# A recurrence's triangular solve spread over more of its group, and the first T of each group placed on chip

## The chip, the cores and the metric

The kernel runs on one core of one Trainium2 chip. The metric is the device time of one execution in microseconds (us). The engines are named as in the profile: PE is TensorE (PEld its weight loads), DVE is VectorE, ACT is ScalarE, POOL is GpSimd, SP is SyncE, which issues most DMAs here.

## What is computed

Three stages follow each other. The first is a recurrence over 768 steps for 4 x 8 heads of 40 x 40 state; the second routes each of the 3072 rows of its output to two of eight experts; the third is a feed-forward layer. The change is in the first alone.

```python
for t in range(S):                      # S = 768
    y[:, :, t] = np.einsum('bhd,bhde->bhe', rt, state)
    Sa = np.einsum('bhde,bhe->bhd', state, at)
    state_decay = state * wt[:, :, None, :] - np.einsum('bhd,bhe->bhde', Sa, bt)
    state = state_decay + np.einsum('bhd,bhe->bhde', vt, kt)
x = y.transpose(0, 2, 1, 3).reshape(B * S, H * D)
x = moe(x)                              # top 2 of 8 experts
return (g(x @ w_in) @ w_out)            # g(h) = h * tanh(softplus(h))
```

## The kernel before, in words

The 768 time steps are cut into 24 chunks of 32 (`C`). Inside a chunk the recurrence becomes matrix products with a triangular 32 x 32 matrix L for each head, and its inverse T. Four chunks (`GJ`) make a group k, and the six groups' T are found by a forward substitution on VectorE, the solve. Five pieces of work run side by side:

- The chain (`chain`), 48 steps, two for each chunk (half of the heads each). A step has on TensorE the products that carry the state (`s_mm`, matmuls cs of ST and KB, L602), two sets of transposes (`tr`, L619), the product u (`u_mm`, L589), the output of the step before (`y_mm`, L559) and rv (`rv_mm`, L634). ScalarE copies u to ST (L592) and the transposes to TRs and KB (L621, L623). VectorE writes RR (L645) and the new ST (L607) for the two steps on.
- The preparation of later chunks (`prepare`): decays E and R, and abd and kb on VectorE (L227 to L240); L (matmuls pp, L280; ACT Ls, L287), stored to the DRAM tile lscr (L288); kn (L314) and EN (L325).
- The solve (`solve_group`), one group ahead of the chunks that need it. SyncE loads L of four chunks from lscr to Lu (L437). VectorE works on Lu and Tt (multiply L466 or L478, sum L468 or L481), and GpSimd takes two of the multiplications. The finished Tt is stored to the DRAM tile tscr (L517).
- The placing of T (`tbd`): T of one chunk is loaded from tscr with four DMAs into the block diagonal of Tbd (L384). There are two Tbd buffers (`NTB`).
- The application (`apply`): TensorE multiplies AM by Tbd (matmuls pp of Tbd and share, L406) and ScalarE copies the result to Zt (L408), which the chain's u needs.

The order of the instructions on each engine is fixed when the program is built. `run` walks through the steps of the chain and, at up to five places in a step (`fill`), issues all side work that is due by then (`pump`). Due times are counted in groups: a group is eight steps. The solve of group k goes from `k - 1 + s[0]` to `k - 1 + s[1]` (`s_1` for k = 1), and its load of Lu is due `ll` = 0.06 ahead. Each engine then takes its instructions in this order and waits where an operand is not ready.

For k = 0 alone, at the start, `own_tbd` makes T of the first chunk without DRAM: VectorE transposes 32 partitions of Tt in 32 x 32 blocks (L374), and ScalarE copies the result to the four diagonal blocks (L378).

Of the kernel before, what the change touches and what calls it, by code (L numbers as in the profile page):

```python
# [24 lines left out]
PR = 8  # L25
NC = S // C
NG = NP * NC
OPT = dict(yd=(), yv=33, gix=(1, 3, 4), ye=(2, 2),  lag2=1, plan=((0, 4, -0.881), (1, 5, -0.7929), (1, 6, -0.7905), (0, 5, -0.3416), (1, 7, -0.3331), (0, 6, -0.2825), (0, 7, -0.1981), (1, 8, -0.1391)), dl=0, dk=0, ns=(0, 0), nw=(1, 1), va=1, rb=0, ra=1, kb=0, ry=(2, 2), p1=(0, 0, 0, 1, 1, 1), lw=((4, 2, 2), (6, 6, 6)), fl=((0, 1, 2, 2, 2, 2, 2, 2), (0,) * 8), lag=6, ll=.06, hurry=40, pool=(1, 4), rvpool=False, f=(3, 3, 1, 1, 1, 0), s=(.05, .72), s_1=(-.12, .62), tl=1.9, zl=.96, zd=.32, t0=-.35, nd=3, z0=8.65)
NW = 2 * PR * (C + 1)
NTB = 2  # L30
GJ = 4
# [34 lines left out]
class Rec:  # L66
# [200 lines left out]
    def prods(self, i):  # L267
# [18 lines left out]
        for out, k in ((ls, 1), (am[:, :, 64:96], 0))[:1 if i < GJ else 2]:  # L286
            nc.scalar.mul(out=out, in_=pv[:, :, k], mul=-1.0)  # L287
        (nc.scalar if i < OPT['dl'] else nc.sync).dma_start(out=self.lscr[i // GJ][i % GJ * PR:i % GJ * PR + PR].rearrange("u q t i -> (q t) u i"), in_=ls)  # L288

# [12 lines left out]
    def turns(self, i):  # L302
# [12 lines left out]
        self.KN[i] = self.pkn.tile([128, HH * D], F32, name="knd")  # L315
        (nc.scalar if i < OPT['dk'] else nc.sync).dma_start(out=self.KN[i], in_=kn.rearrange("p h d -> p (h d)"))
        if i % 2 == 0:
# [28 lines left out]
    def prepare(self):  # L346
        n = len(self.seq)
        for first, i, at in OPT["plan"]:
            yield at
            for k, _ in enumerate((self.decayed if first else self.turned)(i)):  # L350
                yield at if first or at < OPT["t0"] else at + .03 * k
        for i in range(2 * GJ, n):
# [14 lines left out]
        for k in range(len(self.seq) // GJ):  # L367
            yield from self.solve_group(k)

    def own_tbd(self):  # L370

        nc = self.nc
        tv = self.ptm.tile([128, C * C], F32, name="tm")
        nc.vector.transpose(out=tv[0:32].rearrange("p (t x) -> p t x", x=32),  # L374
                            in_=self.Tt[0:32, 0:C * C].rearrange("p (j t) -> p t j", t=C))
        for q in range(4):
            r = slice(32 * q, 32 * q + 32)
            nc.scalar.copy(out=self.Tbd[0][r, :, r], in_=tv[0:32].rearrange("p (t u q) -> p q u t", u=PR, q=4)[:, q])  # L378

    def tbd(self, i):  # L380

# [5 lines left out]
    def apply(self):  # L387

        nc = self.nc
        for i in range(len(self.seq)):  # L390
            at = 2 * i - OPT["zl"]
            if i and i % GJ == 0:
                yield self.tau(2 * i - OPT["tl"])
                self.tbd(i)
            self.wants[2] = lambda: 2 if self.solved <= i // GJ else self.ready <= i
            z = self.Z[(i + 2) % 3]
            am, T = self.AM[i % (2 * GJ)], self.Tbd[i % NTB]
            if i < GJ:
                yield self.tau(at) if i else self.early(OPT['z0'])
                self.halves(i, am, T)  # L400
                T = self.IG
            for sg in range(2):
                yield self.tau(at + sg * OPT["zd"]) if i else self.early(OPT['z0'])
                pt = self.pp.tile([128, 512], F32, name="pp")
                for p in range(4):
                    nc.tensor.matmul(pt[0:96, p * 128:p * 128 + 128], lhsT=am[:, sg * 4 + p],  # L406
                                     rhs=T[:, sg * 4 + p, :], start=True, stop=True)
                nc.scalar.copy(out=z[0:96, sg * 4:sg * 4 + 4].rearrange("p a x -> p (a x)"), in_=pt[0:96])  # L408
            self.ZT[i] = z
            if 0 < i % GJ < GJ - 1 or i and i % GJ == 0:  # L410
                self.tbd(i + 1)
# [28 lines left out]
    def solve_group(self, k):  # L440

        nc = self.nc
        done = [0.0]

        def at(cost):

            done[0] += cost
            if k == 0:
                return self.early(done[0] - cost)
            return s0 + (s1 - s0) * (done[0] - cost) / 21.0  # L450

        s0, s1 = (k - 1 + x for x in OPT["s"]) if k != 1 else OPT["s_1"]
        if k:
            self.wants[1] = lambda: self.made < GJ * (k + 1)
            yield s0 - OPT["ll"]
            self.load_l(k)
        Tt, Lu = self.Tt, self.Lu
        q, h = C // 2, C // 4
        blk = lambda t: t[:, 0:4 * (h * C + h)].rearrange("p (b x) -> p b x", b=4)[:, :, 0:h * C].rearrange(
            "p b (j t) -> p b j t", t=C)  # L460
        Tb, Lb = blk(Tt), blk(Lu)
        for t in range(1, h):
            yield at(.38 + .0083 * t * t)
            tm = self.ptm.tile([128, 2 * C * q], F32, name="tm")
            tm = tm[:, 0:4 * t * t].rearrange("p (b j i) -> p b j i", b=4, j=t)
            nc.vector.tensor_tensor(out=tm, in0=Tb[:, :, 0:t, 0:t],  # L466
                                    in1=Lb[:, :, t, None, 0:t].to_broadcast([128, 4, t, t]), op=ALU.mult)
            nc.vector.tensor_reduce(out=Tb[:, :, 0:t, t:t + 1], in_=tm, axis=AX.X, op=ALU.add)  # L468
        T2 = Tt[:, 0:C * C].rearrange("p (j t) -> p j t", t=C)
        L2 = Lu[:, 0:C * C].rearrange("p (t i) -> p t i", i=C)  # L470
        P = self.one.tile([128, q, q], F32, name="P")
        work, tms = {}, {}

        def mul(i, eng=nc.vector):
            sh, x, y, _ = work[i]
            tm = self.ptm.tile([128, 2 * C * q], F32, name="tm")
            tms[i] = tm[:, 0:sh[0] * sh[1] * sh[2]].rearrange("p (a b c) -> p a b c", a=sh[0], b=sh[1])
            eng.tensor_tensor(out=tms[i], in0=x.to_broadcast([128, *sh]), in1=y.to_broadcast([128, *sh]), op=ALU.mult)  # L478

        def add(i):  # L480
            nc.vector.tensor_reduce(out=work[i][3], in_=tms.pop(i), axis=AX.X, op=ALU.add)  # L481


        for b in range(2):
            o = b * q
            p = P[:, 4 * b:4 * b + 4].rearrange("p a (c x) -> p (a c) x", x=h)
            work[b] = ((h, h, h), T2[:, o:o + h, None, o:o + h], L2[:, None, o + h:o + q, o:o + h], p[:, :, :, None])
            work[2 + b] = ((h, h, h), T2[:, o + h:o + q, o + h:o + q].rearrange("p i t -> p t i")[:, None],
                           p[:, :, None, :], T2[:, o:o + h, o + h:o + q, None])
        for i in range(0, 4, 2):  # L490
            for f in (mul, add):
                for b in range(2):
                    yield at(.6)
                    f(i + b)

        tt = self.T22
        for n, (j0, j1, i0) in enumerate(((0, 4, 0), (4, 8, 0), (8, 16, 8)) if k else ()):
            work[n] = ((j1 - j0, q, q - i0), T2[:, j0:j1, None, i0:q], L2[:, None, q:C, i0:q], P[:, j0:j1, :, None])
        for n, (t0, t1, j0, j1) in enumerate(((8, 16, 0, 8), (8, 16, 8, 16), (0, 8, 0, 16)) if k else ()):
            nt = t1  # L500
            work[3 + n] = ((j1 - j0, t1 - t0, nt),
                           tt[:, None, t0:t1, 0:nt], P[:, j0:j1, None, 0:nt], T2[:, j0:j1, q + t0:q + t1, None])
        pool = OPT["pool"] if k else ()
        for i in range(2 if k else 0):
            yield at(.1 if i in pool else 1.2)
            mul(i, nc.gpsimd if i in pool else nc.vector)
        for i in range(6 if k else 0):
            yield at(1.2)
            add(i)
            if i == 1:  # L510
                nc.scalar.copy(out=tt, in_=T2[:, q:C, q:C].rearrange("p i t -> p t i"))

            for j in {0: [2], 2: [4, 3], 3: [5]}.get(i, []):
                yield at(.1 if j in pool else 1.2)
                mul(j, nc.gpsimd if j in pool else nc.vector)
        self.tscr[k] = self.pd.tile([GJ * PR, 4, C, C], F32, name="tscr")
        (nc.sync if k else nc.scalar).dma_start(out=self.tscr[k].rearrange("u q j t -> (u q) (j t)"), in_=self.Tt[:, 0:C * C])  # L517
        self.solved += 1
        if k == 0:
            self.own_tbd()  # L520
            self.tbd(1)


# [1241 lines left out]
```

## Time and profile before

| | |
|---|---|
| median of 3 runs | 1275.37 us (1272.05 to 1279.73) |
| profiled execution, its own time | 1278.76 us |
| its span, first to last instruction | 1277.0 us |
| mean granted TensorE clock | 0.947 |
| busy in the span: PE, PEld, DVE, ACT, POOL | 1148.3, 1097.6, 857.5, 724.0, 533.4 us |

A busy share is a mean over the three stages. The recurrence takes about the first 450 us, the experts the time up to about 905 us, the feed-forward layer the rest. "Round" means eight steps of the chain, from the start of one `s_mm` to that of the eighth after it: 57.0 to 148.8 us is the round in which group k = 1 is solved, 148.8 to 218.4 k = 2, 218.4 to 288.0 k = 3, 288.0 to 367.5 k = 4, 367.5 to 423.7 k = 5.

### The profile page before, as it was taken

Reading aid. Unit: us, or ns where it says so; the run is one execution under the profiler, and the core shown is the slowest. Engines: PE = TensorE matmul, PEld = TensorE weight load, DVE = VectorE, ACT = ScalarE, POOL = GpSimd, SP = SyncE. Lnnn points to the kernel's source line nnn. Section 1 sums busy time; section 2 is a strip of 40 time slices with the busy share of each in tenths; the row PEclk is TensorE's granted clock in tenths of the full one; section 3 lists DMA queues with packets and bytes.
Section 4 is the critical chain, followed back from the end, with each engine's and each line's share of the span. In section 5 each row is a group of like instructions: output and inputs, shape, how many; then the busy total and the mean of one; then the engine's idle time right before and its main releaser. Section 6 shows DMA issues by size and latency. Waiting matters only on the chain. (4 is left out here: it accounts for less than half of the span.)

```text
span 1277.0 us, 34710 instructions
## 1 busy us (share of the span) xinstructions
PE 1148.3 (90%) x14222; PEld 1097.6 (86%) x14222; DVE 857.5 (67%) x1610; ACT 724.0 (57%) x1517; POOL 533.4 (42%) x518
## 2 busy tenths in 40 slices
PE   6578878887877978999999999989989999999998
PEld 5477767776867868999999999989889999999998
DVE  8769697878956527558778778684466665655543
ACT  6756767766765654424434434333566666666664
POOL 6325332322635145413345344443365555543331
PEclk9688999988989977999999999989999999999999
DMA  9775867665366583645366365662541111110000
GB/s 239 195 180 135 216 159 184 170 177 153 86 120 125 105 134 120 164 141 168 94 187 192 113 190 159 207 194 75 159 112 32 31 32 34 38 34 12 12 11 21
DMA packets 143904, 156.73 MB, mean 123 GB/s; under 512 B 69867, under 2 KB 112875, under 8 KB 143723
## 3 DMA queue, kind: packets, MB, share of 16 engines
q1 hardware_dynamic: 126362, 119.86, 36.7%
q0 software_dynamic: 10752, 22.32, 6.7%
q10 hardware_dynamic: 6608, 12.06, 3.2%
q8 instruction: 122, 2.00, 0.7%
q14 instruction: 60, 0.48, 0.1%
HBM read 111.07 MB, written 43.12 MB: 121 GB/s over the span
## 5 line engine op out<-in xcount | busy, mean ns | idle before, releaser
L1637 POOL TENSOR_TENSOR gl<-fh,gh 128x1024 fp32r<-128x1024 f32 x46 | 131.1, 2878 | 105.3 <-ACT gh L1653 102.0
L1292 PE MATMUL ph<-xh,w1h 128*128 128x256 f32 (+1 forms) x576 | 159.4, 290 | 2.5 <-issue 2.5
L1292 PE MATMUL ph<-xl,w1h 128*128 128x256 f32 (+1 forms) x576 | 159.1, 289 | 0.0
L1605 PE MATMUL fps<-fxh,ih 128*128 128x256 f32 x576 | 156.4, 286 | 1.8 <-DVE fh L1607 1.8
L1605 PE MATMUL fps<-fxl,ih 128*128 128x256 f32 x576 | 153.8, 281 | 0.5 <-DVE fxl L1148 0.3
L1636 DVE TENSOR_TENSOR fh<-fh,fp 128x1024 f32<-128x1024 f32 x48 | 95.0, 2014 | 60.5 <-ACT fp L1635 60.5
L1311 PE MATMUL py<-w2h,hh 128*128 128x320 f32 x400 | 131.2, 328 | 4.3 <-ACT hh L1144 3.5
L1311 PE MATMUL py<-w2h,hl 128*128 128x320 f32 x400 | 127.0, 318 | 1.6 <-DVE hl L1146 1.6
L1311 PE MATMUL py<-w2l,hh 128*128 128x320 f32 x400 | 126.7, 317 | 2.0 <-DVE w2l L1148 1.9
L1146 DVE SCALAR_TENSOR_TENSOR hl<-ph,hh 128x512 fp32r<-128x512 f32 (+1 forms) x104 | 69.2, 665 | 82.6 <-ACT hh L1144 82.3
L1607 DVE COPY fh<-fps 128x512 f32<-128x512 f32 x96 | 64.8, 689 | 79.5 <-ACT fp L1606 74.1
L1667 PE MATMUL fpy<-oh,gl 128*128 128x320 f32 x384 | 114.6, 310 | 0.0
L1667 PE MATMUL fpy<-oh,gh 128*128 128x320 f32 x384 | 114.3, 310 | 0.0
L1667 PE MATMUL fpy<-ol,gh 128*128 128x320 f32 x384 | 113.9, 308 | 0.0
L1292 PEld LDWEIGHTS ph<-xh,w1h 128*128 128x128 f32 x576 | 111.2, 193 | 2.8 <-issue 2.7
L1292 PEld LDWEIGHTS ph<-xl,w1h 128*128 128x128 f32 x576 | 111.2, 193 | 0.3 <-DVE xl L1148 0.3
L1292 PE MATMUL ph<-xh,w1l 128*128 128x256 f32 (+1 forms) x384 | 111.0, 289 | 0.0
L1605 PEld LDWEIGHTS fps<-fxh,ih 128*128 128x128 f32 x576 | 109.0, 189 | 2.1 <-DVE fh L1607 2.0
L1605 PEld LDWEIGHTS fps<-fxl,ih 128*128 128x128 f32 x576 | 109.0, 189 | 1.1 <-DVE fxl L1148 1.1
L1605 PE MATMUL fps<-fxh,il 128*128 128x256 f32 x384 | 107.8, 281 | 0.0
L1144 ACT ACTIVATE hh<-ph 128x512 fp32r<-128x512 f32 (+1 forms) x104 | 59.9, 580 | 81.1 <-PE ph L1292 78.2
L1606 ACT ACTIVATE fp<-fps 128x512 f32<-128x512 f32 x96 | 56.1, 597 | 79.1 <-PE fps L1605 73.5
(299 smaller groups left out, 3215.5 us busy)
## 6 DMA issues: line engine op xcount, KB each, us to landing
share<-in_w_dram SPq DMA_DIRECT2D x9, 1280.0 KB
share<-in_w_dram SPq DMA_DIRECT2D x9, 1024.0 KB
wa<-in_wa_dram SPq DMA_DIRECT2D x40, 195.2 KB
knd<-kn SPq DMA_DIRECT2D x24, 320.0 KB
kb<-in_kb_dram SPq DMA_DIRECT2D x40, 192.0 KB
KB<-knd SPq DMA_DIRECT2D x24, 320.0 KB
yb<-y SPq DMA_DIRECT2D x22, 320.0 KB
ST<-in_vn_dram SPq DMA_DIRECT2D x48, 128.0 KB
```

Of the source, the lines that this page charges most:

```text
L1144: nc.scalar.activation(out=hi, in_=src, func=AF.Relu if relu else AF.Copy)
L1146: nc.vector.scalar_tensor_tensor(out=lo, in0=src, scalar=0.0, in1=hi.bitcast(F32), op0=ALU.max, op1=ALU.subtract)
L1292: nc.tensor.matmul(ph[:, m % c], lhsT=a, rhs=b, start=(q == 0), stop=(q == len(ops) - 1))
L1311: nc.tensor.matmul(py, lhsT=a[:, m, ts], rhs=b[:, m], start=(m == 0 and q == 0), stop=(m == FC - 1 and q == 2))
L1605: nc.tensor.matmul(ph[:, i], lhsT=a, rhs=b, start=(q == 0), stop=(q == len(ops) - 1))
L1606: nc.scalar.activation(out=p[:, 2 * m2:2 * m2 + 2], in_=ph, func=AF.Sigmoid, scale=-1.0)
L1607: nc.vector.tensor_copy(h[:, 2 * m2:2 * m2 + 2], ph)
L1636: mul = lambda s: nc.vector.tensor_tensor(out=h[:, s], in0=h[:, s], in1=p[:, s], op=ALU.mult)
L1637: low = lambda s: (nc.vector if last and s.start % 8 else nc.gpsimd).tensor_tensor(out=gl[:, s], in0=h[:, s], in1=gh[:, s].bitcast(F32), o ...
L1667: nc.tensor.matmul(py, lhsT=a[:, m, ts], rhs=w[:, m], start=(q == 0), stop=(q == len(ops) - 1))
```

## The change

Three things change. The solve's due times: `s` goes from (.05, .72) to (-.06, .75), so that the solve's operations, and the load of Lu ahead of them, start 0.11 of a group (about one step) earlier and end 0.03 later; for k = 1 `s_1` goes from (-.12, .62) to (-.12, .75). `own_tbd` is called at the end of each group's solve, for every k, and writes T of the group's first chunk to Tbd. And the four DMAs that placed this T for k = 1 to 5, with their due time (`tl`), go. T of the other three chunks of a group is loaded from tscr as before.

```diff
-OPT = dict(yd=(), yv=33, gix=(1, 3, 4), ye=(2, 2),  lag2=1, plan=((0, 4, -0.881), (1, 5, -0.7929), (1, 6, -0.7905), (0, 5, -0.3416), (1, 7, -0.3331), (0, 6, -0.2825), (0, 7, -0.1981), (1, 8, -0.1391)), dl=0, dk=0, ns=(0, 0), nw=(1, 1), va=1, rb=0, ra=1, kb=0, ry=(2, 2), p1=(0, 0, 0, 1, 1, 1), lw=((4, 2, 2), (6, 6, 6)), fl=((0, 1, 2, 2, 2, 2, 2, 2), (0,) * 8), lag=6, ll=.06, hurry=40, pool=(1, 4), rvpool=False, f=(3, 3, 1, 1, 1, 0), s=(.05, .72), s_1=(-.12, .62), tl=1.9, zl=.96, zd=.32, t0=-.35, nd=3, z0=8.65)
+OPT = dict(yd=(), yv=33, gix=(1, 3, 4), ye=(2, 2),  lag2=1, plan=((0, 4, -0.881), (1, 5, -0.7929), (1, 6, -0.7905), (0, 5, -0.3416), (1, 7, -0.3331), (0, 6, -0.2825), (0, 7, -0.1981), (1, 8, -0.1391)), dl=0, dk=0, ns=(0, 0), nw=(1, 1), va=1, rb=0, ra=1, kb=0, ry=(2, 2), p1=(0, 0, 0, 1, 1, 1), lw=((4, 2, 2), (6, 6, 6)), fl=((0, 1, 2, 2, 2, 2, 2, 2), (0,) * 8), lag=6, ll=.06, hurry=40, pool=(1, 4), rvpool=False, f=(3, 3, 1, 1, 1, 0), s=(-.06, .75), s_1=(-.12, .75), tl=1.9, zl=.96, zd=.32, t0=-.35, nd=3, z0=8.65)
...
-    def own_tbd(self):
+    def own_tbd(self, k):
...
-            nc.scalar.copy(out=self.Tbd[0][r, :, r], in_=tv[0:32].rearrange("p (t u q) -> p q u t", u=PR, q=4)[:, q])
+            nc.scalar.copy(out=self.Tbd[GJ * k % NTB][r, :, r], in_=tv[0:32].rearrange("p (t u q) -> p q u t", u=PR, q=4)[:, q])
...
-            if i and i % GJ == 0:
-                yield self.tau(2 * i - OPT["tl"])
-                self.tbd(i)
...
         self.solved += 1
+        self.own_tbd(k)
         if k == 0:
-            self.own_tbd()
             self.tbd(1)
```

What stands on the engines shows three places. Lines behind 394 have a number lower by three in the changed kernel. First VectorE where the solve of k = 3 begins (the first operations on Lu); before:

```order
L645 TENSOR_TENSOR RR_247<-cs,mrv 64x256 x2
L607 TENSOR_TENSOR ST_160<-cs,WE 40x8x40 x2
L236 TENSOR_TENSOR abd_167<-wa_140,E 104x512
L240 TENSOR_TENSOR kb_143<-kb_143,R 104x1024
L466 TENSOR_TENSOR tm<-Tt,Lu 128x4
L468 TENSOR_REDUCE Tt<-tm 128x4
```

and in the changed kernel:

```order
L642 TENSOR_TENSOR RR_247<-cs,mrv 64x256 x2
L604 TENSOR_TENSOR ST_164<-cs,WE 40x8x40 x2
L463 TENSOR_TENSOR tm<-Tt,Lu 128x4
...
L465 TENSOR_REDUCE Tt<-tm 128x4x4
L227 SCALAR_TENSOR_TENSOR E<-wa_140,d_155 104x528
L230 RECIPROCAL d1b<-E 104x16
L231 SCALAR_TENSOR_TENSOR R<-wa_140,d1b 104x529
L642 TENSOR_TENSOR RR_247<-cs,mrv 64x256 x2
L604 TENSOR_TENSOR ST_160<-cs,WE 40x8x40 x2
```

The first operation on Lu has moved ahead of the E and R of a chunk, the pair that writes ST_160, and abd and kb: one step of the chain. The second place is ScalarE at the end of the same solve (second half of a Zt, then EN, TRs, KB and the copies of u to ST); before:

```order
L408 COPY Zt_212<-pp 96x512
L325 COPY EN<-pp 64x4x2x40
L621 COPY TRs<-cs 128x256
L623 ACTIVATE KB_137<-cs 40x4x40 x2
L592 COPY ST_162<-cs 32x8x40 x2
```

and in the changed kernel:

```order
L405 COPY Zt_212<-pp 96x512
L378 COPY Tbd_209<-tm 32x8x32 x4
L325 COPY EN<-pp 64x4x2x40
L618 COPY TRs<-cs 128x256
L620 ACTIVATE KB_137<-cs 40x4x40 x2
L589 COPY ST_162<-cs 32x8x40 x2
```

The four copies to Tbd stand ahead of the second EN of the step, and all that follows on ScalarE is queued behind them. On VectorE the transpose stands directly behind the two last reductions of the solve, which follow the pair that writes ST_164, as before. The third place is SyncE ahead of the solve of k = 3; before, from the store of tscr of k = 2 on:

```order
L517 DMA tscr<-Tt 128x1024
...
L547 DMA rbd_241<-in_r_dram 48x512 x2
L384 DMA Tbd_209<-tscr 32x8x32 x4
L288 DMA lscr<-Ls 128x8x32
...
L541 DMA RR_243<-in_rt_dram 48x1024
L384 DMA Tbd_210<-tscr 32x8x32 x4
L205 DMA kb_141<-in_kb_dram 48x1024 x2
L257 DMA AT<-in_at_dram 64x640
L527 DMA KB_138<-knd 64x2x640
L437 DMA Lu<-lscr 128x1024
```

and in the changed kernel:

```order
L514 DMA tscr<-Tt 128x1024
...
L544 DMA rbd_241<-in_r_dram 48x512 x2
L288 DMA lscr<-Ls 128x8x32
...
L538 DMA RR_243<-in_rt_dram 48x1024
L434 DMA Lu<-lscr 128x1024
L384 DMA Tbd_210<-tscr 32x8x32 x4
```

The four loads of Tbd_209 are gone, and the load of Lu has moved ahead of Tbd_210, kb, AT and KB.

## Rows read from the trace of the kernel before

**Rows 1.** Windows by round: length, busy us of PE, PEld, DVE, ACT, POOL, clock.

```profile
218.40:288.00 69.60, 58.94 (x1383) 52.26 (x1381) 55.45 (x84) 48.89 (x136) 23.16 (x19) 0.93 0.69 174
288.00:367.50 79.50, 62.36 (x1386) 55.77 (x1384) 57.53 (x113) 49.17 (x135) 29.17 (x27) 0.85 0.51 126
```

**Rows 2.** Waits, 57 to 452 us: total us, times, longest.

```profile
DVE tm L466 <- DMA Lu<-lscr: 22.4, 4, 8.1
PE pp L406 <- DMA Tbd<-tscr: 12.5, 4, 6.4
```

**Rows 3.** Timeline of VectorE, round of k = 3: start, us, operation [idle before].

```profile
227.24 0.32 DVE L466 TENSOR_TENSOR tm<-Tt,Lu 128x4 f32<-128x4 f32 x1 [4.82 <-DMA Lu<-lscr]
...
265.43 0.86 DVE L645 TENSOR_TENSOR RR<-cs,mrv 64x256 f32<-64x256 f32 x2
266.32 0.99 DVE L607 TENSOR_TENSOR ST<-cs,WE 40x320 f32<-40x320 f32 x2
267.23 2.33 DVE L481 TENSOR_REDUCE Tt<-tm 128x64 f32<-128x1024 f32 x2
269.48 1.24 DVE L227 TENSOR_TENSOR_SCAN E<-wa,d 104x528 f32<-104x528 f32 x1
...
271.05 1.26 DVE L231 TENSOR_TENSOR_SCAN R<-wa,d1b 104x529 f32<-104x529 f32 x1
...
274.14 0.68 DVE L236 TENSOR_TENSOR abd<-wa,E 104x512 f32<-104x512 f32 x1
...
274.74 1.21 DVE L240 TENSOR_TENSOR kb<-kb,R 104x1024 f32<-104x1024 f32 x1
```

**Rows 4.** Timeline of VectorE, solve of k = 4: first and last operation.

```profile
296.04 0.17 DVE L466 TENSOR_TENSOR tm<-Tt,Lu 128x4 f32<-128x4 f32 x1 [4.05 <-DMA Lu<-lscr]
...
345.99 1.21 DVE L481 TENSOR_REDUCE Tt<-tm 128x128 f32<-128x1024 f32 x1
```

**Rows 5.** Timeline at the end of the solve of k = 0.

```profile
42.88 1.92 DVE L374 STREAM_TRANSPOSE tm<-Tt 32x1024 f32<-32x1024 f32 x1
...
44.84 2.59 ACT L378 COPY Tbd<-tm 32x256 f32<-32x256 f32 x4 [0.41 <-DVE tm L374]
```

**Rows 6.** Timeline of ScalarE at the end of the solve of k = 3.

```profile
266.95 0.42 ACT L325 COPY EN<-pp 64x320 f32<-64x320 f32 x1
...
267.32 0.37 ACT L621 COPY TRs<-cs 128x256 f32<-128x256 f32 x1
...
267.59 0.61 ACT L623 ACTIVATE KB<-cs 40x160 f32<-40x160 f32 x2
...
268.23 0.86 ACT L592 COPY ST<-cs 32x320 f32<-32x320 f32 x2
```

**Rows 7.** Timeline of TensorE: two starts of a step, two waits for T.

```profile
262.17 1.28 PE L602 MATMUL cs<-ST,KB 128*40 128x40 f32 x32
...
269.42 0.81 PE L602 MATMUL cs<-ST,KB 128*40 128x40 f32 x32
...
281.24 1.99 PE L406 MATMUL pp<-Tbd,share 128*96 128x128 f32 x8 [2.21 <-DMA Tbd<-tscr]
...
359.19 1.99 PE L406 MATMUL pp<-Tbd,share 128*96 128x128 f32 x8 [6.44 <-DMA Tbd<-tscr]
```

**Rows 8.** Timeline of SyncE's queue, end of k = 2 to the load of k = 3.

```profile
200.59 0.34 SPq L517 DMA_DIRECT2D tscr<-Tt  x1
...
205.65 2.49 SPq L384 DMA_DIRECT2D Tbd<-tscr  x4
...
212.56 0.64 SPq L541 DMA_DIRECT2D RR<-in_rt_dram  x1
...
220.24 0.58 SPq L437 DMA_DIRECT2D Lu<-lscr  x1
```

**Rows 9.** Windows behind two waits for T: columns as in rows 1, clock third last.

```profile
281.20:284.60 3.40, 3.36 (x18) 3.35 (x19) 1.55 (x3) 1.00 (x2) 0.00 (x0) 0.56 0.94 298
359.20:363.00 3.80, 3.80 (x20) 3.76 (x21) 0.00 (x0) 1.19 (x3) 0.00 (x0) 0.54 0.85 204
```

## The prediction

> **What bounds the kernel now.** I read the table of windows first, then the waits, then the timelines of VectorE, ScalarE, TensorE and SyncE around one end of a solve. The change touches only the recurrence, some 57 to 450 us of the span; what follows starts from its results, so a gain there is a gain at the end. In the round of eight steps from 218.4 to 288.0 [rows 1] no engine is full: TensorE 58.94 of 69.60 us, VectorE 55.45, ScalarE 48.89. The round is a chain with two nearly full engines, and which of them waits changes inside it. VectorE's first operation of the solve starts at 227.24, 8.8 us into the round, after 4.82 us of idling for Lu, and its last one (the second of a pair of reductions, 267.23 + 2.33) ends at 269.56 [rows 3]. Between the two it is packed: 42.3 us without a gap worth naming. So from 227 to 270 VectorE leads and TensorE follows; after that, until the next solve begins at 296.04 [rows 4], VectorE waits. T is late as well: TensorE waited 12.5 us in four waits for Tbd, VectorE 22.4 us in four for Lu [rows 2], and the T waits shown are 2.21 us and 6.44 us [rows 7].
>
> **The change, part by part.** *The T waits go.* They are worth 12.5 us of idle TensorE [rows 2]. The round trip was: the store of Tt to tscr, 4 placing DMAs (2.49 us of SyncE's time [rows 8]), landing. In its place VectorE turns 32x1024 in 1.92 us and ScalarE copies four blocks in 2.59 us [rows 5], so T lies ready 4.5 us after the solve's end.
>
> *What is put on the engines, and who waits.* Per group VectorE gets 1.92 us and ScalarE 2.59 us. Both stand in queues that run in order. The order of ScalarE shows the four copies behind the second Zt copy and ahead of EN, TRs, KB and the copies to ST. Now those run at 266.95, 267.32, 267.59 and 268.23, taking 0.42, 0.37, 0.61 and 0.86 us [rows 6], and the next step's first matmuls (ps of KB and ST) start at 269.42 [rows 7]. Put D for the end of the transpose: 269.56 + 1.92 = 271.5 at today's pace. ScalarE would stand still from 267.0 to D, copy until D + 2.6, and the matmuls could start at D + 2.6 + 0.4 + 0.4 + 0.6 + 0.9 + 0.3 = D + 5.2 = 276.7 in place of 269.4. That is 7.2 us later in one step, more than the 2.21 us that the T wait of this round costs. It is the term that the change's own words don't tell. It cannot be hidden by the work behind it on ScalarE, because the u copies to ST in it are what the chain waits for.
>
> *What the spreading gives back.* The first operations now stand one step earlier, directly behind the ST products of the round before. One more step's work of VectorE lies inside the stretch of the solve: an RR and ST pair (265.43 to 267.23, 1.8 us), an E and R (269.48 to 272.31, 2.83 us) and an abd and kb (274.14 to 275.95, 1.8 us) [rows 3], 6.5 us together. So the packed stretch becomes 42.3 + 1.9 + 6.5 = 50.8 us (rounded), while the idle stretch behind it shrinks. How far it shrinks is the open size. Now it is 26.5 us (269.56 to 296.04) [rows 3, 4]. The load of Lu is issued at 220.24 and lands for 227.24, 7.0 us; it follows the store of tscr at 200.59 by 19.65 us [rows 8]. In the new order it stands right behind the load of RR, which ends its issue at 212.56 + 0.64; it passes the rows from there to 220.24 (7.0 us), and the four Tbd issues ahead (2.49 us) are gone. If nothing on SyncE waits, Lu is issued 19.65 - 9.5 = 10.2 us after the solve's end, that is at D + 8.2, and is there at D + 15. But the RR load, the store of L and others wait for what ScalarE and TensorE free, and these are 7 us later than now; D + 22 is the other bound. I take D + 17, nearer to the lower one, because the issues between can overlap the stall.
>
> *Weighed against a rule.* After the 6.44 us wait TensorE ran at a granted 0.54 for 3.8 us and after the 2.21 us wait at 0.56 for 3.4 us, at or near the lower of its levels (1.2 of 2.4 GHz) [rows 9]; 3.8 us at 0.54 cost 1.7 us of work. The Trainium skill, "TensorE: Matmul & The Clock Gate", Part 1, says that the clock follows how busy the engine has been, and its section on loop structure calls a long wait between matmuls the bad form. By that rule the new wait cools TensorE as the old one does, five times in place of four, and the sum below would be 1.7 us higher; the rows agree as far as they go.
>
> **The sum**, against the profiled execution (1278.8 us, span 1277.0; the median of the runs, 1275.4, is 3.4 us lower).
> - Rounds of k = 2 and k = 3, 69.6 us each [rows 1] (k = 2 is the same pattern): 50.8 + 17 = 67.8, so -1.8 us each, -3.6. This holds the stall and the T wait that goes; bounds -3.8 each (D + 15) and +3.2 each (D + 22).
> - Round of k = 4, 79.5 us [rows 1]: VectorE's stretch is longer here, since routing lies in it, 296.04 to 347.20 = 51.2 us [rows 4], and becomes 51.2 + 8.4 = 59.6. A round starts two steps behind the stall, each 7.25 us (262.17 to 269.42) [rows 7], so at D + 5.2 + 14.5 = D + 19.7; Lu at D + 17 is 2.7 us ahead of the round. The round is -2.7 + 59.6 + 19.7 = 76.6: -2.9 us, with the 6.44 us T wait gone in it. Bounds -5 and +2.
> - Round of k = 1: it has no T wait now (the four are those of k = 2 to 5) and gets transpose, copies and stall. Its start is not moved, only its end, by one step. Between 0 (hidden) and +7.2 I take +3.
> - Round of k = 5: stall +7.2; the T wait left of the 12.5 (12.5 - 2.2 - 6.4 = 3.9 for k = 2 and 5; 1.7 if k = 2 is like k = 3) and the low clock behind it (1.7 [rows 9]) go, and the solve starts a step earlier in a round without preparation work, where VectorE is packed at the front only. I take 0, between -6 and +5.
> - SyncE's 2.49 us a group are in D + 17; that DMA traffic is 4 x 32 KB less per group I cost at nothing, since the transfers that the chain waits for here are waited for by order and latency; if it shortens the landing of Lu by 1 us, it is 3 us in the three rounds.
> Together -3.6 - 2.9 + 3 + 0 = -3.5: 1275.3 us profiled, and a median of **about 1272 us**. That is 0.3% and inside the 0.5% which a measurement here can tell from no change.
>
> **The rivals.**
> 1. *The stall is hidden, and the steps even out.* If VectorE, less packed, is never behind its ST products, a round would be eight steps of 7.25 us and the stall: 58 + 5.2 = 63.2 us. VectorE's own sum, 55.45 + 1.92 = 57.4 us [rows 1, 5], allows it. For it: the packed stretch has now its longest steps while two light steps follow. Against: a step's share of the solve stays near TensorE's step, so one late result holds both. -6.4 twice, -6 in k = 4 and +3 in k = 1 give -16: 1259 us. Chance 0.25.
> 2. *Slower: ScalarE blocked by the transpose.* Place: the four copies at the head of ScalarE's queue, five times. Price: if Lu comes at D + 21, the rounds are 71.8 us (+2.2 twice), k = 4 is +1.1, k = 1 +7.2, k = 5 +5: +17.7, or 1293 us. It decides from D + 18.8 on, where 50.8 + 18.8 reaches today's 69.6; or when the copies come up more than 4 us ahead of the transpose's end in the rounds that have no long T wait to give. For it: in rows 6 and 3 ScalarE is there 4.5 us early. A lower clock behind each stall [rows 9] adds to it. Chance 0.18.
> 3. *Nothing moves.* The earlier place in the queue is only an earlier wait: Lu lands when the chain lets L be stored, VectorE waits in front of its first operation as long as it starts earlier (more than the 4.82 us of now), and copies and T waits cancel. 1275 us, chance 0.12.
>
> **How the numbers follow.** The forecast has a chance of 0.45 and its own range of 1265 to 1280; 0.10 of it lies under 1269 (faster by 0.5%), 0.33 between, 0.02 above 1281.7. Rival 1 adds 0.25 to faster, rival 2 adds 0.18 to slower, rival 3 0.10 to same and 0.01 to each side. So faster 0.36, same 0.43, slower 0.21. For 8 in 10 the range leaves out about a tenth on each side: 1257 to 1288.
>
> **What would show it.** Right: no wait of TensorE on Tbd at the end of a group; ScalarE idle 3 to 5 us ahead of the copies from tm, released by VectorE's transpose, with TensorE idle and a lower granted clock behind it; the solve's first operation near the start of a round in place of 8.8 us into it, with its Lu wait still there; rounds near 68, 68 and 77 us. Wrong: rounds near 63 us with copies that wait for nothing (rival 1); a wait for Lu above 6 us in each round, or a first round over 5 us longer (rival 2). The prediction is wrong at its root if the stretch from the first operation to the end of the solve is no longer packed, because then 50.8 is no floor for it.

## The result, and the profile after

The changed kernel took 1291.82 us (median of 5 runs, 1285.29 to 1292.26) beside 1275.37 us of the kernel before on the same chip: 1.0112 times as long, 95% interval 1.0087 to 1.0138. It is slower by 1.1%; the forecast of 1272 us and its range to 1288 were wrong, and the time that came is that of rival 2 (1293 us). The profiled execution is the fastest of the five: 1285.29 us, span 1283.5. TensorE is as busy in it as before (1149.6 us, before 1148.3); VectorE (865.8 us, before 857.5) and ScalarE (736.5, before 724.0) are busier by about the added work.

The first view is the table of windows, one row for each of the five rounds, with the columns of [rows 1] (behind the clock stand the busy share of the DMA engines and the GB/s that they moved).

```profile
57.10:152.60 95.50, 76.77 (x1810) 68.23 (x1810) 68.36 (x93) 62.81 (x171) 28.79 (x24) 0.86 0.69 166
152.60:226.90 74.30, 61.78 (x1386) 54.34 (x1381) 56.91 (x85) 51.45 (x139) 25.19 (x20) 0.89 0.67 165
226.90:298.90 72.00, 58.65 (x1384) 50.95 (x1380) 57.67 (x85) 51.44 (x139) 25.07 (x19) 0.93 0.65 165
298.90:380.50 81.60, 63.92 (x1388) 56.66 (x1384) 61.89 (x120) 51.97 (x139) 27.81 (x27) 0.83 0.49 117
380.50:435.50 55.00, 45.24 (x1061) 41.02 (x1061) 38.08 (x64) 37.20 (x101) 26.92 (x37) 0.91 0.61 103
```

Before, the rounds were 91.8, 69.6, 69.6, 79.5 and 56.2 us long, 366.7 in all. They are now +3.7, +4.7, +2.4, +2.1 and -1.2: 378.4, or +11.7. The span grew by only 6.5 because the rest of this execution was 5.3 us shorter (848.0 us in place of 853.3). In a second profiled execution of the changed kernel (the first run of the second series) the rounds are +15.2, the span +14.1 and the rest 852.4 us, so the 5.3 us of the rest did not come again and the loss lies in the rounds.

The second view is the list of waits from 57 to 440 us (total us, times, longest).

```profile
POOL share L264 <- ACT EN L325: 66.8, 10, 14.4
DVE tm L463 <- DMA Lu<-lscr: 28.3, 5, 8.3
PE cs L631 <- ACT TRs L618: 22.0, 4, 7.2
ACT Tbd L378 <- DVE tm L374: 21.9, 5, 5.4
```

The 12.5 us of TensorE on Tbd [rows 2] are gone. In their place ScalarE waits 21.9 us for the five transposes, TensorE 22.0 us for ScalarE's TRs, and GpSimd's product of AT and EN (`share`) waits 66.8 us for ScalarE, 48.4 before. The waits for Lu have not become shorter: 28.3 us in five, 22.4 in four before. The third view is the timeline around the end of the solve of k = 3, engine by engine; it answers to [rows 3] and [rows 5 to 8].

```profile
276.28 1.89 DVE L374 STREAM_TRANSPOSE tm<-Tt 32x1024 f32<-32x1024 f32 x1
...
273.42 0.58 ACT L405 COPY Zt<-pp 96x512 f32<-96x512 f32 x1
278.20 2.56 ACT L378 COPY Tbd<-tm 32x256 f32<-32x256 f32 x4 [4.20 <-DVE tm L374]
280.79 0.42 ACT L325 COPY EN<-pp 64x320 f32<-64x320 f32 x1
281.11 0.36 ACT L618 COPY TRs<-cs 128x256 f32<-128x256 f32 x1
281.38 0.61 ACT L620 ACTIVATE KB<-cs 40x160 f32<-40x160 f32 x2
282.01 0.86 ACT L589 COPY ST<-cs 32x320 f32<-32x320 f32 x2
...
281.53 1.11 PE L631 MATMUL cs<-rbd,TRs 128*64 128x64 f32 x14 [5.99 <-ACT TRs L618]
283.40 1.30 PE L599 MATMUL cs<-ST,KB 128*40 128x40 f32 x32
...
292.69 0.81 PE L599 MATMUL cs<-ST,KB 128*40 128x40 f32 x32
...
281.29 1.79 POOL L264 TENSOR_TENSOR share<-AT,EN 64x320 f32<-64x320 f32 x2 [8.48 <-ACT EN L325]
...
276.71 1.18 SPq L205 DMA_DIRECT2D kb<-in_kb_dram  x2
283.11 0.47 SPq L257 DMA_DIRECT2D AT<-in_at_dram  x1
...
288.89 0.42 SPq L1712 DMA_DIRECT2D xd<-X  x1
292.11 0.34 SPq L316 DMA_DIRECT2D knd<-kn  x1
...
293.50 0.40 SPq L434 DMA_DIRECT2D Lu<-lscr  x1
```

Read it from the transpose on. It ends at D = 276.28 + 1.89 = 278.17. ScalarE had been free since 274.0, stood 4.20 us, and copied until 280.8. Behind it EN, TRs, KB and ST follow, TensorE resumes at 281.53 after 5.99 us, and the next `s_mm` is at 283.40, D + 5.2. The stall does not end there. GpSimd's product of EN comes at 281.29 and frees AT at 283.08; SyncE stands in front of the load of AT from 277.9 on and issues it at 283.11; at 289.3 it stops again, for kn, which ScalarE has copied by 292.08, and goes on at 292.11; and Lu, behind all of it, is issued at 293.50, D + 15.3.

The next rows are VectorE's transposes and the first operations on Lu of the groups around them.

```profile
153.82 0.26 DVE L463 TENSOR_TENSOR tm<-Tt,Lu 128x4 f32<-128x4 f32 x1 [6.21 <-DMA Lu<-lscr]
...
204.11 1.89 DVE L374 STREAM_TRANSPOSE tm<-Tt 32x1024 f32<-32x1024 f32 x1
227.17 0.30 DVE L463 TENSOR_TENSOR tm<-Tt,Lu 128x4 f32<-128x4 f32 x1 [4.65 <-DMA Lu<-lscr]
...
299.09 0.40 DVE L463 TENSOR_TENSOR tm<-Tt,Lu 128x4 f32<-128x4 f32 x1 [4.55 <-DMA Lu<-lscr]
...
356.41 1.89 DVE L374 STREAM_TRANSPOSE tm<-Tt 32x1024 f32<-32x1024 f32 x1
379.33 0.30 DVE L463 TENSOR_TENSOR tm<-Tt,Lu 128x4 f32<-128x4 f32 x1 [4.62 <-DMA Lu<-lscr]
```

From D to the next solve it is 227.17 - 206.00 = 21.2 us, 299.09 - 278.17 = 20.9 and 379.33 - 358.30 = 21.0, and VectorE waits for Lu each time. In the second profile of the changed kernel it is 19.7, 22.7 and 20.6. From the first operation to D it is 206.00 - 153.82 = 52.2 us for k = 2, 278.17 - 227.17 = 51.0 for k = 3 and 358.30 - 299.09 = 59.2 for k = 4.

### The profile page after: what moved, and what is told of

Its sections match the earlier page's. It is cut to its first block, busy times and chain, and to the rows that moved or that the text cites. A ratio compares the mean times of both kernels' runs of the same rounds, so it can differ in the third digit from the quotient of the medians.

```text
span 1283.5 us, 34709 instructions
## 1 busy us (share of the span) xinstructions
PE 1149.6 (90%) x14222; PEld 1097.1 (85%) x14222; DVE 865.8 (67%) x1615; ACT 736.5 (57%) x1537; POOL 528.2 (41%) x518
## 5 line engine op out<-in xcount | busy, mean ns | idle before, releaser
L264 POOL TENSOR_TENSOR share<-AT,EN 64x320 f32<-64x320 f32 x48 | 51.4, 1072 | 154.5 <-issue 79.9
```

What stands on the lines that cost most here:

```text
L264: self.nc.gpsimd.tensor_tensor(out=self.AM[i % (2 * GJ)][64 * ab:64 * ab + 64, :, 0:D], in0=self.AT[r, ab], in1=en[r, ab], op=ALU.mult)
```

## The experiments

The 16 runs came in four series, each on another chip; the kernel before was timed in each (1302.65, 1275.89, 1277.36 and 1307.3 us), and a run is judged by its ratio to it in its own series. A difference of two ratios of one series is marked as on one chip.

| run | what stands in it | ratio | 95% interval |
|---|---|---|---|
| e1_chip_only | T on chip, old times | 1.0185 | 1.0130 to 1.0239 |
| e2_spread_only, e9_spread_again | new times, T through DRAM | 0.9974, 0.9993 | 0.9938 to 1.0009, 0.9969 to 1.0018 |
| e3_copies_late, e14_late_again | both, copies late, ahead of rxt | 1.0004, 0.9999 | 0.9975 to 1.0032, 0.9970 to 1.0028 |
| e4_late_old_times | as e3, old times | 1.0047 | 1.0021 to 1.0073 |
| e5_after_again | the changed kernel | 1.0114 | 1.0078 to 1.0150 |
| e6_gpsimd_copies | both, copies on GpSimd | 1.0033 | 1.0009 to 1.0056 |
| e7_copies_behind_rxt, e10_rxt_again, e15_rxt_third | both, copies late, behind rxt | 0.9920, 0.9938, 0.9965 | 0.9892 to 0.9947, 0.9911 to 0.9966, 0.9937 to 0.9994 |
| e8_end_only | later end alone, T through DRAM | 1.0023 | 0.9997 to 1.0050 |
| e11_rxt_old_times | as e10, old times | 1.0056 | 1.0030 to 1.0082 |
| e12_rxt_wider | as e10, solve to 0.81 | 0.9917 | 0.9884 to 0.9950 |
| e13_at_gpsimd | changed kernel, AT loaded from GpSimd | 1.0112 | 1.0074 to 1.0149 |
| e16_rxt_at_gpsimd | as e15, AT loaded from GpSimd | 0.9943 | 0.9912 to 0.9974 |

My theory was that ScalarE's stall is the loss (A). The rivals: that the spreading itself loses (B), and that the added work of VectorE and ScalarE does, wherever it waits (C).

**One part at a time.** The changed kernel with the old due times, and the kernel before with the new ones:

```diff
-OPT = dict(..., s=(-.06, .75), s_1=(-.12, .75), ...)     # e1; e2 is the reverse, in the kernel before
+OPT = dict(..., s=(.05, .72), s_1=(-.12, .62), ...)
```

> The change with the old due times (s and s_1 as before), T of each group's first chunk still turned and placed on chip. Theory A, ScalarE's stall: the loss comes from the four copies that wait in front of ScalarE's queue for VectorE's transpose (about 5 us of step time in each of five groups, against 12.5 us of T waits that go). Then this alone is slower than before, 1283 to 1298 us, with ScalarE waits for the transpose of 3 to 7 us. Theory B, the spreading: the earlier and longer solve puts VectorE work ahead of RR and ST and loses by itself. Then this kernel, without it, is as before or faster, 1262 to 1277 us.

> The kernel before with the new due times alone, T placed through DRAM as before. Theory A: faster than before or the same, 1260 to 1277 us, since no copy waits on ScalarE; the waits for T may grow a little, as the solve ends 0.17 step later. Theory B: slower, 1283 to 1295 us, with longer waits for Lu or for RR.

T on chip alone is 1.0185, the spreading alone 0.9974. In the first, ScalarE waits 21.8 us in four for the transposes and TensorE 32.6 us in seven for TRs. The loss comes with the T on chip and the same wait of ScalarE, and not with the spreading; B falls. What the spreading does alone is small: the waits for T fall from 12.5 to 6.7 us and those for Lu rise from 22.4 to 39.6 us.

**The copies late.** The transpose stays where it is; the four copies of k = 1 to 5 are due 1.15 steps ahead of their chunk's own step in the chain. The matmul that needs them is due 0.96 ahead of that step, so the copies stand 0.19 of a step in front of it, by when the transpose is done. (The kernels with late copies have the transpose in L374 as before, these copies in L385, and the lines behind them with numbers higher by ten than in the changed kernel.)

```diff
-            nc.scalar.copy(out=self.Tbd[GJ * k % NTB][r, :, r], in_=...)   # in own_tbd
+            if i and i % GJ == 0:
+                yield self.tau(2 * i - OPT["tl"])        # tl=1.15
+                self.place(i // GJ)                      # the same four copies
```

> The change with its transpose where it is, but the four copies on ScalarE issued about 1.3 steps later, behind the copies of u to ST of the next step and a quarter step ahead of the product that needs T. Theory A: the wait in front of ScalarE's queue is gone, the copies' 2.5 us stay; 1262 to 1277 us, TensorE waiting neither for T nor 6 us for TRs. Theory B: as the change, 1283 to 1295 us. Theory C, that the added work itself (1.9 us of VectorE and 2.5 us of ScalarE a group) is the loss: 1282 to 1292 us as well, but with no wait of the copies.

> As e3, but with the old due times. Theory A: near or under before, 1266 to 1278 us, the T waits gone and no stall. Theory B: faster than e3 by 8 us or more, as the spreading is away too. Theory C: as e3, 1282 to 1292 us.

With the copies late none of them waits, and the ratio falls from 1.0112 to 1.0004 at the new times, from 1.0185 to 1.0047 at the old: 1.1% (across two chips) and 1.4% (on one), some 14 and 18 us. That is theory A. But both stayed above the same kernel with T through DRAM, by 0.3% (the intervals overlap) and 0.5%, so a part of C was open. The timeline of TensorE and ScalarE in e3 showed where:

```profile
144.11 1.58 PE L946 MATMUL pp<-wgn,rxt 128*128 128x16 f32 x6 [6.55 <-ACT rxt L933]
...
141.12 2.55 ACT L385 COPY Tbd<-tm 32x256 f32<-32x256 f32 x4
143.69 0.37 ACT L933 COPY rxt<-pp 128x256 f32<-128x256 f32 x1
```

The copies don't wait any more, but stand ahead of rxt (a piece of the output, turned for the routing), for which TensorE's queue waits with `s_mm` behind it.

**The place of the copies, and another engine.** In the second series the changed kernel ran again, then with the copies on GpSimd, then with the late copies one place further on, then the kernel before with the later end alone.

> The changed kernel again, beside the next three and on their chip. Theory A (ScalarE stands still in front of the four copies) and theory C (the added work itself) both say that the loss does not depend on the chip: 1.011 of the time of the kernel before, between 1.008 and 1.014. The rival: on another chip the last steps of the recurrence hold a wait that hides or doubles a part of it, as in the four runs ahead of this one; then the ratio is under 1.006 or over 1.016.

The loss came again, 1.0114.

```diff
-            nc.scalar.copy(out=self.Tbd[GJ * k % NTB][r, :, r], in_=...)
+            (nc.gpsimd.tensor_copy if k else nc.scalar.copy)(out=self.Tbd[GJ * k % NTB][r, :, r], in_=...)
```

> The changed kernel with the four copies to Tbd on GpSimd for k = 1 to 5, at the same place in the program, directly behind the transpose. GpSimd may wait for the transpose without holding the chain. If ScalarE is the whole cause (its wait and its 2.5 us of copies), TensorE's waits for TRs go (22 us in four to under 5), the steps of 13.6 to 16.8 us go back to some 9, and the ratio is 0.995 to 1.000, near the 0.9974 of the spreading alone. If the transpose on VectorE (1.9 us a group, ahead of E and R) holds the chain as well, 5 x 1.9 = 9.5 us stay: 1.002 to 1.006. No row shows such a copy on GpSimd; if its four take over 8 us, TensorE waits for Tbd again.

TensorE's waits for TRs fell to 5.0 us at most, but the ratio only to 1.0033. This is the timeline of GpSimd and SyncE in it, at the end of k = 3:

```profile
279.58 4.42 POOL L378 COPY Tbd<-tm 32x256 f32<-32x256 f32 x4 [7.32 <-DVE tm L374]
284.08 3.47 POOL L264 TENSOR_TENSOR share<-AT,EN 64x320 f32<-64x320 f32 x2
...
277.97 2.11 SPq L205 DMA_DIRECT2D kb<-in_kb_dram  x2
287.57 0.47 SPq L257 DMA_DIRECT2D AT<-in_at_dram  x1
...
294.57 0.37 SPq L434 DMA_DIRECT2D Lu<-lscr  x1
```

Now GpSimd stands for 7.32 us with its product of EN behind the copies, SyncE stands from 280.1 to 287.57 with its load of AT, and Lu is late: 49.3 us of waits for it in five, 13.3 at most. The stall moved to another queue. By the expectation 1.0033 could also be the transpose's time on VectorE; the next run keeps that transpose and is faster than the kernel before, so the transpose alone does not explain it. (This trace is of an execution of 1268.8 us; the median is 1278.46.)

```diff
-OPT = dict(..., tl=1.15, ...)     # copies late; the matmul that needs them is due at 0.96
+OPT = dict(..., tl=1.0, ...)
```

> The kernel with late copies (e3_copies_late) with their due time moved from 1.15 to 1.0 steps ahead of the matmul of T, so that they stand behind the copies to rxt and not ahead of them. In e3_copies_late the copies stood at 141.12 us for 2.55 us, rxt came behind them at 143.69, and TensorE, idle from 137.6, waited 6.55 us for rxt at 144.11; the first two rounds were 96.7 and 73.8 us, against 92.2 and 70.9 of the spreading alone. If the place of the copies is what is left of the loss, the first two rounds come back by 2.5 us or more each and the ratio goes from 1.0004 to 0.996 to 0.998. If it is the 1.9 us of VectorE, they stay and the ratio is 1.000 within its interval.

> The kernel before with the later end of the solve alone: s from (.05, .72) to (.05, .75) and s_1 from (-.12, .62) to (-.12, .75); T through DRAM, and the load of Lu at its old place. The spreading alone had 39.6 us of waits for Lu in five, the kernel before 24.8. If the earlier start only buys a longer wait for Lu, and the gain is the later end's, the ratio is that of the spreading alone or better, 0.994 to 0.998, with waits for Lu near 25 us. If the earlier start is what gains, it is 0.999 to 1.003.

The copies behind rxt gave 0.9920, faster than both kernels and below the 0.996 that I had expected at best; against the changed kernel (e5) that is 1.9% on one chip. Its rounds are 94.8, 68.5, 68.2, 73.7 and 55.1 us, 360.3 in all, where e5 has 381.9. TensorE waits 2.4 us for rxt, 6.6 in e3, and 3.8 us in three for the copies themselves. The first round stays 3 us longer than before; the transpose, with its 1.9 us, stands there ahead of E, but no run tells how much of the 3 us it is. The later end alone (e8) gained nothing (1.0023): T through DRAM then came late, 20.1 us of waits for it in four, with 21.4 for Lu. By the expectation that leaves the earlier start as the part that gains, but no run has it alone.

**On one chip: spreading, T on chip, and both.**

> The spreading alone, T through DRAM, again (0.9974, 0.9938 to 1.0009, on another chip), beside the next three. If T on chip is itself worth something once its copies hold nobody up, the next run is faster than this one by over 0.3%; if the placing on chip is worth nothing and the spreading is the whole gain, the two are equal, near 0.994.

> The changed kernel with its copies behind rxt, again: 0.992 (0.9892 to 0.9947) the first time. If that was the place of the copies, it comes again, 0.989 to 0.996. The rival: the gain came from the luck of a chip, and it is 0.997 to 1.001, like the copies ahead of rxt.

> T on chip with its copies behind rxt, and the due times of the kernel before. In the pairs so far the spreading gave 0.3 to 0.7%. If it still does with the copies out of the way, this is 0.995 to 0.999 where the run with both is 0.992. If the spreading only serves to hide a stall that is no longer there, it equals the run with both.

```diff
-OPT = dict(..., s=(-.06, .75), s_1=(-.12, .75), ...)     # e10
+OPT = dict(..., s=(-.06, .81), s_1=(-.12, .81), ...)     # e12
```

> The same as the run with copies behind rxt, but the solve ends at 0.81 of a group in place of 0.75: its last reduction moves one step on, and the transpose with it, so that it lies ahead of abd and kb in place of E and R. T is needed about a step behind. If more spreading is more gain, 0.986 to 0.991. If T comes too late, the copies wait for the transpose again and TensorE for Tbd (over 3 us a group), and the ratio is 0.995 or more.

The spreading alone is 0.9993, T on chip alone 1.0056, both 0.9938 and, still wider, 0.9917 (its interval overlaps that of e10). Neither part gains alone, both together do: the spreading is worth 1.2% with T on chip and nothing measurable without, and T on chip gains 0.5% with the spreading and loses 0.6% without. In e9 waits for T (9.1 us in three) and for Lu (42.1 in five) remain. In e11 the rounds of k = 2 to 4 were 215.1 us (218.7 before), the first 93.3 (91.8) and the fifth 63.5 (56.2), with 6.8 us in front of an `s_mm` for which the trace names no cause (2.9 us in the same step before, 3.2 in e10); why T on chip loses there stays open.

**What holds Lu.** I thought that SyncE's wait for GpSimd, ahead of the load of AT, was what brought the stall to Lu. In e13 the loads are issued from GpSimd's own queue:

```diff
-            self.nc.sync.dma_start(out=self.AT[r:r + 64]...
+            (self.nc.sync if i < 2 else self.nc.gpsimd).dma_start(out=self.AT[r:r + 64]...
```

> The changed kernel with the loads of AT (L257, from the third on) issued from GpSimd's queue, directly behind the two products that free the buffer, in place of SyncE's. SyncE then has no wait for GpSimd ahead of the load of Lu. If the stall comes back through SyncE, Lu is issued near D + 10 in place of D + 15.3 in the round of k = 3, the first operation of the solve starts at D + 15 to D + 17, and the rounds of k = 2, 3 and 4 are some 4 us shorter each (12 us, 0.9%): 1.000 to 1.005 of the kernel before, with ScalarE's waits for the transpose still there. If other waits on SyncE (knd for kn, kb for abd) hold Lu as long, it stays at D + 19 or later and the ratio at 1.008 to 1.014.

> Late copies, ahead of rxt, again (1.0004 on another chip), beside the next run. If the place ahead of rxt is what it lost against the copies behind rxt, it is 0.998 to 1.003 here; if the chip made the difference, 0.991 to 0.996, equal to the next.

> Late copies behind rxt, a third time (0.992 and 0.9938): 0.990 to 0.996 if it holds on any chip; 0.998 to 1.002 if this chip is like the first.

> Late copies behind rxt and the loads of AT from GpSimd's queue. Without the stall Lu was issued at D + 9.35 in the round of k = 3 and waits for AT are no longer behind a held ScalarE; so the loads from GpSimd should bring little: 0.989 to 0.994, equal to the run without. If SyncE's wait for GpSimd holds Lu without the stall too, Lu comes 2 us or more earlier and the ratio is 0.985 to 0.989.

That theory fell: e13 gave 1.0112. SyncE's queue in e13, at the end of k = 3 (the transpose ends at 275.5):

```profile
274.04 1.19 SPq L205 DMA_DIRECT2D kb<-in_kb_dram  x2
280.96 0.58 SPq L524 DMA_DIRECT2D KB<-knd  x1
...
286.19 0.37 SPq L1712 DMA_DIRECT2D xd<-X  x1
292.55 0.34 SPq L316 DMA_DIRECT2D knd<-kn  x1
...
293.93 0.40 SPq L434 DMA_DIRECT2D Lu<-lscr  x1
```

The wait for AT is gone, and the next load, KB, waits 5.7 us in its place, then knd 6.0 us for kn; Lu is issued at D + 18.4, as in the second profile of the changed kernel (296.53, with D at 278.18). Each of them needs something that stands behind the copies on ScalarE. Without the stall (e10) SyncE stops nowhere for over 1 us in this stretch; VectorE and SyncE there:

```profile
269.84 1.95 DVE L374 STREAM_TRANSPOSE tm<-Tt 32x1024 f32<-32x1024 f32 x1
286.03 0.17 DVE L473 TENSOR_TENSOR tm<-Tt,Lu 128x4 f32<-128x4 f32 x1 [3.51 <-DMA Lu<-lscr]
...
281.12 0.39 SPq L444 DMA_DIRECT2D Lu<-lscr  x1
```

D is 271.79, Lu is issued at D + 9.3 and the solve starts at D + 14.2. So it is the stall that holds Lu, through whichever load stands first on SyncE; the lower clock behind the stall adds to it (below). The loads of AT alone bring nothing measurable without the stall either (0.9943 beside 0.9965). On this chip copies ahead of rxt gave 0.9999 and behind it 0.9965, with intervals that overlap; all three runs behind rxt lie under both runs ahead of it, so the place is worth 0.3 (on one chip) to 0.8% (across two).

## Why the prediction was wrong

- **The T waits go**: right, all 12.5 us.
- **ScalarE's copies hold the chain**: right, and to the tenth for k = 2 and 3: `s_mm` at D + 5.2. It is D + 4.3 in k = 4, D + 5.4 in k = 5 and D + 10.0 in k = 1, where TensorE's queue stands for EN. ScalarE is there 3.0 to 5.4 us ahead of the transpose's end, 4.2 in k = 3 (4.5 read from rows 3 and 6). D + 5.2 is 7.3 us behind 269.42, not 7.2, which changes nothing. The runs with late copies give its price, 1.1 to 1.4%.
- **The packed stretch of VectorE** of 50.8 us (its parts add up to 50.7) and 59.6 in k = 4: right, 51.0 and 59.2 (52.2 in k = 2).
- **"I take D + 17, nearer to the lower one, because the issues between can overlap the stall"**: this is the step that failed. D + 17 is an issue of Lu at D + 10 and 7.0 us until the solve starts on it. Lu was issued at D + 15.3 to D + 15.7 and the solve started 5.4 to 5.7 us behind that, at D + 20.9 to D + 21.2: the issue was over 5 us later than assumed, the landing about 1.4 us shorter. SyncE's issues don't overlap the stall: in k = 3 it stands 5.2 us for AT and 2.8 us for kn, both held up by the stall, and without these 8.0 us Lu would be at D + 7.3, near the D + 8.2 of the lower bound (D + 9.3 in e10). The steps were too short as well: I counted two of 7.25 us from D + 5.2 on; they took 9.3 us (283.40 to 292.69) and 6.2, so the round of k = 4 began at D + 20.7. Of the 15.2 us between the forecast's rounds (-3.5) and the measured (+11.7), k = 2 has 6.5, k = 3 4.2 and k = 4 5.0; in k = 2, 4.2 of it is D + 21.2 and 1.4 its stretch of VectorE, in k = 3, 3.9 of it is D + 20.9.
- **k = 1 (+3) and k = 5 (0)**: +3.7 and -1.2 (+3.5 and -0.8 in the second profile), inside their bounds. Both were taken from the middle of wide bounds, so that is luck as much as reckoning.
- **The clock** was weighed at 1.7 us and left out of the sum; it is part of the miss, most plainly in the second profile. In the 3.8 us behind the stall, 281.5 to 285.3, TensorE was granted 0.59 and in the next 4.1 us 1.00, near the two levels. In the second profile of the same kernel it was granted 0.50 in both, though busy for all but 0.04 us of them. The step behind the stall took 12.7 us there (283.42 to 296.07) in place of 9.3, Lu was issued at D + 18.4 in place of D + 15.3, and the round of k = 3 was 75.6 us in place of 72.0. The Trainium skill, "TensorE: Matmul & The Clock Gate", Part 1, says that the clock follows how busy the engine has been; the low clock behind the wait agrees, but busy time by the profile does not tell these two executions apart. First the two stretches in the first profile, then the same and the two `s_mm` in the second:

```profile
281.50:285.30 3.80, 3.77 (x97) 3.19 (x101) 1.38 (x4) 2.56 (x7) 1.51 (x2) 0.59 0.21 49
285.30:289.40 4.10, 3.90 (x87) 3.26 (x75) 2.17 (x3) 3.51 (x13) 1.48 (x1) 1.00 0.93 238
...
281.50:285.30 3.80, 3.76 (x75) 3.18 (x79) 1.37 (x4) 2.57 (x7) 1.51 (x2) 0.50 0.26 56
285.30:289.40 4.10, 4.10 (x63) 3.89 (x54) 2.19 (x3) 2.67 (x9) 0.73 (x1) 0.50 0.94 240
...
283.42 1.30 PE L599 MATMUL cs<-ST,KB 128*40 128x40 f32 x32
296.07 0.81 PE L599 MATMUL cs<-ST,KB 128*40 128x40 f32 x32
...
296.53 0.40 SPq L434 DMA_DIRECT2D Lu<-lscr  x1
```

- **Rival 2** named place and price (1293 us, 1291.82 measured), and its turning point at D + 18.8 agrees with the runs: D + 20.9 and more lost, D + 14.2 (e10) gained. Its sum fits better than its parts: k = 3 was 71.8 us (72.0 measured), but k = 1 came at +3.7 and not +7.2, k = 5 at -1.2 and not +5, and k = 2 at +4.7 and not +2.2. Its own signs did not come: the first round is 3.7 us longer and not over 5, and the waits for Lu are 4.6 us in the last three rounds and not above 6 in each. I gave it 0.18 because I placed Lu near an empty SyncE, though I had written myself that its loads wait for what ScalarE and TensorE free. **Rival 1** (rounds of 63 us, no stall) came for no kernel; without the stall and with the copies behind rxt the rounds of k = 2 and 3 are 67 to 70 us, and 64.3 at the least (k = 3 in e12). **Rival 3** fell with the interval.

## What to carry to other kernels

A copy that waits on an engine with its queue in order costs not its own 2.6 us but all that stands behind it, and the loads that need what stands behind it: issue it when its operand is there, and look what it stands ahead of. A stall isn't overlapped by a DMA queue whose loads wait for the stalled engine; follow one load from its issue back to that engine before giving it a latency. One half of a change may show no gain by itself where both halves together gain: here 0.35 to 0.8% once the copies were out of the way. And a wait on TensorE may cost more than its own length, because a lower clock can follow it, for a time that differs from execution to execution.

## What the runs showed of the hardware

The same copy took GpSimd 0.61 to 0.63 us or about 1.5 us, in one group of four. In e6 at the end of k = 3 the first two, at 279.58 and 281.12, ran beside the two scans of VectorE on wa and the last two beside RR and ST, whose operand cs is in PSUM:

```profile
279.58 1.48 POOL L378 COPY Tbd<-tm 32x256 f32<-32x256 f32 x1 [7.32 <-DVE tm L374]
281.12 2.88 POOL L378 COPY Tbd<-tm 32x256 f32<-32x256 f32 x3
...
279.45 1.20 DVE L227 TENSOR_TENSOR_SCAN E<-wa,d 104x528 f32<-104x528 f32 x1
280.98 1.26 DVE L231 TENSOR_TENSOR_SCAN R<-wa,d1b 104x529 f32<-104x529 f32 x1
282.27 0.86 DVE L642 TENSOR_TENSOR RR<-cs,mrv 64x256 f32<-64x256 f32 x2
```

The Trainium skill, "SBUF — State Buffer", SBUF: two separate sides, says that a GpSimd operation that reads SBUF and a VectorE operation with two inputs in SBUF lock one pair of ports against each other; these rows agree (in the group of k = 4, with RR and ST alone beside them, all four took 0.61 to 0.63 us). So an engine that looks idle, GpSimd at 41% of the span, is no cheap place for a copy that VectorE's scans run beside.
